# Three-product mix in float32 for the first batch, earlier transforms of the next batch, and a split load before the first product

## Chip, cores and metric

One NeuronCore of one Trainium2 chip runs the whole program. The metric is the device time in microseconds (us) of one execution. Times inside the program are microseconds from the start of the profiled execution's span.

## What is computed

```python
X = np.fft.rfft(x, axis=1)                 # x: 8 batches, 3072 rows, 256 channels, float32
Xr, Xi = X.real, X.imag
Yr = Xr @ w_r - Xi @ w_i + b_r             # the complex "mix", 256x256
Yi = Xr @ w_i + Xi @ w_r + b_i
Y  = softshrink(Yr, 0.01) + 1j * softshrink(Yi, 0.01)
y  = np.fft.irfft(Y, n=3072, axis=1)
out = ((y @ w_a) * (y @ w_b)) @ w_out      # w_a, w_b: 256x1536, w_out: 1536x256, 64-bit floats
```

`w_a`, `w_b` and `w_out` arrive as 64-bit floats; VectorE (DVE) and ScalarE (ACT) decode them from their 32-bit words inside the kernel.

## The kernel before

**Stages.** The transform of 3072 rows is factored in two steps (48 by 64). For each batch `b` the program has: `f1`, 16 tasks that multiply a block of `x` by a 96x96 matrix and store it to DRAM (`g_d`); `f2` and `f3`, 12 tasks each (index `u`), the second transform step and the mix; `i1`, 12 tasks, the first step of the inverse, stored to DRAM (`d_d`); and `i2`, which loads `d_d` back (`dt`) and makes the rows `yr` that enter the products. The products run over 32 pairs of row blocks and, in each, 12 blocks `j` of the hidden width; `step` does one `j`: seven products (Strassen-Winograd, `prod(p, j, k)`, k = 0 to 6) and four pieces of the projection (`proj`). Tasks of the next batch are put into two `slot()` places of each step.

**Number formats.** Batches 1 to 7 split each operand in a high and a low float32r part (`split`: ACT makes the high part, DVE or GpSimd (POOL) the low part) and multiply three times (`mm3`). Batch 0 goes in plain float32 on TensorE (PE), with one pass less of preparation: `f3_plain` multiplies the real and the imaginary part (`X[:, dh, i]`) each by a 512 column matrix (`wab`), and adds the bias by float32r products of `pick` with `bias_k` (tile name `early`).

**The startup** is everything before step 0: load, `f1` of batch 0, `f2`/`f3`/`i1` of batch 0, and meanwhile the decoding of four chunks of `w_a`, `w_b` (`in_weights`, tiles `w_t`, `w`, results `wc0` to `wc3`) and of four blocks of `w_out` (`out_weights(j)`, j = 0 to 3, results `wo0` to `wo3`). Each `out_weights(j)` is a chain: ACT takes the absolute value, six DVE operations, ACT casts the high part, and one more subtraction gives the low part.

**Order.** No engine reorders. The class `Order` decides in which order instructions are written to each engine: it keeps a planned time for PE and the other engines and writes an operation of a chain when its planned time has come. `od.put(c)` writes all that is left of chain `c` at once. `spare` chains are written only where the plan has room. `od.without = "G"` keeps POOL out of the choice.

**End of the startup.** After the last `i1`, PE runs 24 products whose result nobody reads (`busy(24, ...)`), then two `f1` tasks of batch 1 (`AHEAD = 2`), then `i2` of the first pair, then step 0. The loads of `dt` wait until the last block of `d_d` has landed. The four `w_out` blocks are all decoded before step 0.

Of the kernel before, what the change touches and what calls it, by code (L numbers as in the profile page):

```python
# [12 lines left out]
F32 = mybir.dt.float32  # L13
# [104 lines left out]
RING = 9  # L118
AHEAD = 2
LATE = 4  # L120
# [144 lines left out]
def fft_mix_glu_kernel(ctx: ExitStack, tc: tile.TileContext, x, w_r, w_i, b_r, b_i, w_a, w_b, w_out, c1, c1f, vf, m2, v, t2, c3, out):  # L265
# [72 lines left out]
    def load_mix():  # L338
        tmp = state["tmp"]
        wab = state["wab"] = [tmp.tile([P, 2, 2 * D], F32, name=f"wab{c}", bufs=1) for c in range(2)]  # L340
        v_f = state["v_f"] = tmp.tile([P, 2, P], F32, name="v_f", bufs=1)
        pick_in = tmp.tile([34, 3, P], F32, name="pick_in", bufs=1)
        bias_in = tmp.tile([34, D], F32, name="bias_in", bufs=1)
        wr, wi = (wab[0][:, :, D * k : D * (k + 1)] for k in range(2))
        wn, wr2 = (wab[1][:, :, D * k : D * (k + 1)] for k in range(2))
        for o, w in ((wr, w_r), (wi, w_i), (wr2, w_r)):
            nc.sync.dma_start(o, w.rearrange("(c p) e -> p c e", p=P))
        nc.vector.memset(bias_in, 0.0)
        nc.vector.memset(pick_in, 0.0)
        for k in (0, 32):  # L350
            for q, bq in enumerate((b_r, b_i)):
                nc.gpsimd.dma_start(bias_in[k + q : k + q + 1], bq[None, :])
            nc.gpsimd.dma_start(pick_in[k : k + 2], c3)
        nc.gpsimd.dma_start(v_f, vf)
        at = od.load(10 * P)
        return od.chain(
            ("A", 512, lambda e: nc.scalar.mul(wn, wi, -1.0)),
            ("AV", 3 * P, lambda e: copy(e, pick, pick_in)),
            ("A", D, lambda e: nc.scalar.copy(bias_k, bias_in)),
            ("V", D, lambda e: tt(e, bias_k[32:34], bias_in[32:34], bias_k[32:34].bitcast(F32), ALU.subtract)),  # L360
            spare=True,
            after=at,
        )

    def split_mix():
        w2, w3, v_in = (p1.tile([P, 2, D], F32, tag=t, name="w_in") for t in ("sxh", "sxl", "xs"))
        v_in = v_in.rearrange("p s (i n) -> p s i n", i=2)
        c1_in = state["tmp"].tile([R, 2, R], F32, name="c1_in", bufs=1)
        wr, wi = (state["wab"][0][:, :, D * k : D * (k + 1)] for k in range(2))
        nc.sync.dma_start(c1_in, c1)  # L370
        nc.sync.dma_start(v_in, v)
        for q, bq in enumerate((b_r, b_i)):
            nc.sync.dma_start(bias[:, q, :], bq[None, :].to_broadcast([P, D]))
        ops = [
            ("V", 512, lambda e: nc.vector.scalar_tensor_tensor(w3, wr, -1.0, wi, op0=ALU.mult, op1=ALU.subtract)),
            ("VG", 512, lambda e: tt(e, w2, wi, wr, ALU.subtract)),
            ("AV", 2 * R, lambda e: copy(e, c1_sb, c1_in)),
        ]
        for k, w in enumerate((wr, w2, w3)):
# [34 lines left out]
    def in_weights(first, last, raw_tile, w_tile, t_tile, deep=1):  # L414
# [26 lines left out]
        def combine(i):  # L441
# [19 lines left out]
            ops += parts((4, b11), (6, b12), (5, b22), (2, b21))  # L461
            chunks[c] = od.chain(*ops, ("S", 0, lambda e: out_weights(0) if c == LATE - 1 else None), spare=True)

# [15 lines left out]
    def out_weights(j):  # L479

        early = j < EARLY
        if j == 0:
            out_load(0)
        elif not early:
            od.put(wo_done[j - 1])
        if j != EARLY - 1:
            out_load(j + 1)
        raw = state.pop(("wo", j))
        if early:
            hi, lo = (p6.tile([P, W], F32, tag="yr", name="w_t")[:, :D] for _ in range(2))  # L490
            w = state["tmp"].tile([P, D], F32, tag="w", name="w", bufs=5)
        else:
            a = p1.tile([P, 2, D], F32, tag="zy", name="wo_a")
            b = p1.tile([P, 2, D], F32, tag="zc", name="wo_b")
            hi, lo, w = a[:, 0], a[:, 1], b[:, 0]
# [22 lines left out]
    def f1_pre(b, u):  # L518
# [6 lines left out]
        xs[b, u] = xh, xl, od.chain(*split(512, xi, xh, xl), after=t if b < 2 else 0.0)  # L525

    def busy(n, l, r):

        for _ in range(n):
            mm(bank[0][: l.shape[1], : r.shape[1]], l, r, True, True)  # L530

# [90 lines left out]
    def f2_plain(u, bk):  # L622

        X = state["tmp"].tile([P, 2, 2, P], F32, tag="ld", name="sf")
        ops = [("AV", 512, lambda e: copy(e, X.rearrange("p dh c n -> p (dh c n)"), bk))]
        Z = X
        if u == 0:
            Z = state["tmp"].tile([P, 2, 2, P], F32, tag="ld", name="sf0")

            def cut(e):  # L630
                nc.vector.tensor_copy(Z, X)
                nc.vector.memset(Z[:, :, :, 0:1], 0.0)

            ops.append(("V", 600, cut))
        c = od.chain(*ops, urgent=len(ops))
        od.reads(bk, c, len(ops) - 1)
        xs[0, u] = X, Z, c

# [3 lines left out]
    def f3_plain(u, i):  # L642
        X, Z, c = xs[0, u]
        if i == 0:
            bk = f3_ps[u] = od.bank()
            od.need(c)
        else:
            bk = f3_ps.pop(u)
        pa, pb = bk[:, 0:D], bk[:, D : 2 * D]
        wab = state["wab"]  # L650
# [4 lines left out]
        if u == 0:
            if i == 0:
                return
            for k, o in ((1, pb), (0, pa)):
                for c_ in range(2):
                    if c_:  # L660
                        biased(o, 2 * k)
                    for dh in range(2):
                        w = wab[c_][:, dh, D * k : D * (k + 1)]
                        mm(o, (X if c_ == k else Z)[:, dh, c_], w, c_ == dh == 0, c_ == dh == 1, skip_group_check=True)
        else:
            for dh in range(2):
                mm(bk, X[:, dh, i], wab[i][:, dh], i == dh == 0, i == dh == 1, skip_group_check=True)
            if i == 0:
                biased(pa, 0)
                biased(pb, 1)  # L670
                return
        xs.pop((0, u))
        if u > 1:
# [3 lines left out]
        lo, hi = slice(0, 64), slice(64, 128)  # L677
        take = [
            ("AV", D, lambda e, o=o, h=h, p=p, q=q: copy(e, y[o, h], p[q]))
            for o, p in ((hi, pb), (lo, pa))  # L680
            for h, q in enumerate((lo, hi))
        ]
        c = od.chain(
            *take,
            ("v", 512, lambda e: nc.vector.tensor_scalar(z, y, LAM, -LAM, op0=ALU.min, op1=ALU.max)),
# [182 lines left out]
    def proj(p, j, i):  # L868
# [183 lines left out]
    with tc.manual_schedule():  # L1052
# [5 lines left out]
        f1_loads(0)  # L1058
        mix = load_mix()
        in_weights(  # L1060
# [17 lines left out]
        ts = first_mid_tasks()  # L1078
        ts[-3] = after(ts[-3], lambda: [f1_loads(1), ms.extend(i2_matrix(0, th) for th in range(2))])
        tasks.extend(ts)  # L1080
        while tasks:
            slot()
        od.put(rest)
        busy(24, v_sb[:, 0, 1], wm_h[:, 0].rearrange("p i d -> p (i d)"))
        od.stored(2 * P)
        for th in range(2):
            i2_load(0, 0, th, ms[th])
        f1_start(1)
        for t in f1_tasks(1)[:AHEAD]:
            t()  # L1090
        for c in range(LATE):
            have(c)
        for j in range(EARLY):
            od.put(wo_done[j])
        od.spare_slack = 0.0
        startup.close()
        od.without, od.pace = "", 2.8
        state["ring"] = pool("ring", RING)
# [90 lines left out]
```

## Time and profile before

| | us |
|---|---|
| three timed runs | 2907.4, 2909.16, 2910.06; median 2909.16 |
| the profiled execution | 2907.86 |
| its span, first to last instruction | 2905.4 |
| PE busy in the span | 2855.6 (98%) |
| DVE, ACT, POOL busy | 1838.1, 1467.4, 817.6 |

The profiled execution is 1.3 us below the median, and 2.5 us of it lie outside the span. PE is busy for 98% of the span, so time is to be had or lost where PE waits or repeats work; the page shows this in the first two of its 40 slices, which are the startup. The table says nothing of single waits; these are in the rows below.

### The profile page before, as it was taken

What the parts mean: (1) busy time and instruction counts of PE and PEld (TensorE: products, weight loads), DVE (VectorE), ACT (ScalarE), POOL (GpSimd) and SP (SyncE); (2) the same over time, 40 slices, a digit from 0 to 9 for tenths busy, and PEclk for the clock granted to TensorE, in tenths of its full rate; (3) what the DMA queues carried; (4) which work ended last, traced back from release to release, by engine and by line L of the source; (5) the groups of instructions that cost most, each with busy time, mean ns of one, the idle gap of its engine ahead of it and who ended that gap; (6) DMA issues with size and microseconds to landing.
All of it is one profiled execution on the core that took longest, in us unless ns stands there. A gap on an engine that the chain in (4) does not pass through costs nothing.

```text
span 2905.4 us, 46403 instructions
## 1 busy us (share of the span) xinstructions
PE 2855.6 (98%) x16837; PEld 2653.8 (91%) x16837; DVE 1838.1 (63%) x3670; ACT 1467.4 (51%) x3205; POOL 817.6 (28%) x762
## 2 busy tenths in 40 slices
PE   6899999999999999999999999999999999999999
PEld 3599999999999999999999999999999999999998
DVE  6776666566666666566665666656666566666665
ACT  4554555545455444545446444464454545444444
POOL 1132332223322323323323233133332233310000
PEclk8999999999999999999999999999999999999999
DMA  7531212211132111321113211131111311110000
GB/s 243 149 99 41 63 37 89 78 38 60 41 100 75 49 44 53 100 63 51 40 58 100 63 54 37 59 98 60 58 40 55 109 45 59 37 52 22 21 12 23
DMA packets 122965, 187.02 MB, mean 64 GB/s; under 512 B 12652, under 2 KB 81360, under 8 KB 122736
## 3 DMA queue, kind: packets, MB, share of 16 engines
q1 hardware_dynamic: 120784, 176.54, 20.0%
q0 software_dynamic: 1840, 7.48, 0.9%
q8 instruction: 132, 2.16, 0.3%
q14 instruction: 97, 0.79, 0.1%
q10 hardware_dynamic: 112, 0.04, 0.0%
HBM read 108.52 MB, written 75.50 MB: 63 GB/s over the span
## 4 chain that ended last, share of the span: by engine, by line
PE 90%; ACT 2%; POOL 1%; DVE 1%; issue 1%; DVEq 0%; ACTq 0%; POOLq 0%
PE bank L299 90%; ACT s L947 1%; DVE bank L293 1%; POOL sx L293 0%; POOL ycl L293 0%; ACT xs L290 0%; POOL xs L293 0%; ACT osb L290 0%; ACT g L922 0%; DVE s L293 0%; ACT zh L408 0%; ACT sx L594 0%; ACT sx L597 0%; ACT g L984 0%; ACT yr L290 0%
## 5 line engine op out<-in xcount | busy, mean ns | idle before, releaser
L293 DVE TENSOR_TENSOR bank<-bank,s 128x384 f32<-128x384 f32 x1152 | 648.6, 563 | 662.6 <-PE bank L299 557.9
L947 ACT COPY s<-bank 128x384 f32<-128x384 f32 x1152 | 549.2, 485 | 210.0 <-PE bank L299 200.3
L984 ACT CAST g<-bank 128x384 fp32r<-128x384 f32 x384 | 184.5, 480 | 830.2 <-DVE s L293 439.0
L293 DVE TENSOR_TENSOR g<-bank,g 128x384 fp32r<-128x384 f32 x768 | 425.8, 556 | 171.0 <-ACT g L984 143.2
L293 DVE TENSOR_TENSOR s<-bank,s 128x384 f32<-128x384 f32 x768 | 423.6, 552 | 12.5 <-PE bank L299 0.8
L293 POOL TENSOR_TENSOR ycl<-yr,ych 128x384 fp32r<-128x384 f32 x194 | 203.2, 1071 | 691.9 <-ACT ych L408 691.5
L922 ACT CAST g<-bank 128x384 fp32r<-128x384 f32 x384 | 184.4, 480 | 214.2 <-DVE bank L293 213.2
L293 POOL TENSOR_TENSOR zy<-zy,zc 128x512 f32<-128x512 f32 x84 | 107.8, 1283 | 544.3 <-DVE zc L742 537.2
L293 POOL TENSOR_TENSOR x<-xin,x 96x512 fp32r<-96x512 f32 x109 | 144.0, 1323 | 397.2 <-ACT x L408 209.5
L299 PE MATMUL bank<-ych,wc0l 128*128 128x384 f32 x672 | 233.0, 347 | 7.2 <-ACT s L947 5.9
L299 PE MATMUL bank<-ych,wc3l 128*128 128x384 f32 x672 | 235.5, 350 | 0.4
L299 PE MATMUL bank<-ych,wc2l 128*128 128x384 f32 x672 | 232.7, 346 | 0.0
L299 PE MATMUL bank<-ych,wc1l 128*128 128x384 f32 x672 | 230.7, 343 | 0.6
L299 PE MATMUL bank<-ycl,wc0h 128*128 128x384 f32 x672 | 226.8, 338 | 0.5 <-POOL ycl L293 0.5
L299 PE MATMUL bank<-ych,wc3h 128*128 128x384 f32 x672 | 226.6, 337 | 0.0
L299 PE MATMUL bank<-ycl,wc2h 128*128 128x384 f32 x672 | 226.6, 337 | 0.0
L299 PE MATMUL bank<-ych,wc2h 128*128 128x384 f32 x672 | 226.5, 337 | 0.0
L299 PE MATMUL bank<-ych,wc0h 128*128 128x384 f32 x672 | 226.5, 337 | 0.0
L299 PE MATMUL bank<-ycl,wc3h 128*128 128x384 f32 x672 | 226.5, 337 | 0.0
L299 PE MATMUL bank<-ycl,wc1h 128*128 128x384 f32 x672 | 226.2, 337 | 0.0
L299 PE MATMUL bank<-ych,wc1h 128*128 128x384 f32 x672 | 226.1, 336 | 0.0
L299 PE MATMUL bank<-wm_h,sx 128*128 128x256 f32 x1008 | 191.3, 283 | 5.1 <-POOL sx L293 5.1
(197 smaller groups left out, 6423.1 us busy)
## 6 DMA issues: line engine op xcount, KB each, us to landing
xin<-in_x_dram SPq DMA_DIRECT2D x128, 192.0 KB, 2.9
g_d<-gst SPq DMA_DIRECT2D x128, 192.0 KB, 2.1
gt<-g_d SPq DMA_DIRECT2D x96, 256.0 KB, 2.8
d_d<-dst SPq DMA_DIRECT2D x96, 256.0 KB, 2.1
dt<-d_d SPq DMA_DIRECT2D x64, 384.0 KB, 4.1
out_dram<-osb SPq DMA_DIRECT2D x64, 384.0 KB, 2.6
m_in<-const_m_dram SPq DMA_DIRECT2D x96, 128.0 KB, 2.1
t_in<-const_t_dram SPq DMA_DIRECT2D x64, 144.0 KB, 2.4
```

The source lines that it names most:

```text
L293: (nc.vector if e == "V" else nc.gpsimd).tensor_tensor(o, a, b, op=op)
L299: nc.tensor.matmul(o, lhsT=l, rhs=r, start=start, stop=stop, **kw)
L922: ("A", W, lambda e: nc.scalar.copy(h, X)),
L947: return s, od.chain(("A", W, lambda e: nc.scalar.copy(s, q[:, :W])), urgent=1)
L984: ("A", W, lambda e: nc.scalar.copy(h1, Y)),
```

## The change

It has five parts.

1. The mix of batch 0 uses three products for a complex multiplication in place of four: `(Xr+Xi) w_r` (its copy on ACT is `k`), `Xr (w_i - w_r)` and `Xi (-w_r - w_i)`, each of 256 columns. DVE makes the sum `Xr+Xi` (`ss`) and adds `k` when it takes two of the four result blocks out of PSUM.
2. `w_r` and `w_i` are loaded once each, by POOL's DMA queue behind the first `w_a`, `w_b` blocks, instead of three loads by SP. The two differences (`w23`) are made in `load_mix` and used again in `split_mix`.
3. `AHEAD` goes from 2 to 6: six `f1` tasks of batch 1 stand before `i2`. The four next ones (`GAP`) go together into the first slot of step 0. `busy` is gone.
4. `dt` is loaded in two parts: rows 0 to 79, and rows 80 to 95, which the last two `i1` tasks write.
5. `out_weights(0)` is started only after the `dt` loads, and `w_out` blocks 0 to 3 are finished by `out_have`, called from step 0 (through `out_weights(4)`), not before `i2`. POOL stays out of the choice until the first pair's parts are split.

```diff
-AHEAD = 2
+AHEAD = 6
+GAP = 4
...
     def load_mix():
...
-        for o, w in ((wr, w_r), (wi, w_i), (wr2, w_r)):
-            nc.sync.dma_start(o, w.rearrange("(c p) e -> p c e", p=P))
+        for o, w in ((wr, w_r), (wi, w_i)):
+            nc.gpsimd.dma_start(o, w.rearrange("(c p) e -> p c e", p=P))
...
     def out_weights(j):
...
         if j == 0:
             out_load(0)
-        elif not early:
-            od.put(wo_done[j - 1])
-        if j != EARLY - 1:
-            out_load(j + 1)
+        else:
+            out_have(j - 1)
+        out_load(j + 1)
...
+    def out_have(j):
+        while j not in wo_done:
+            od.put(wo_done[max(wo_done)])
+        od.put(wo_done[j])
...
     def f3_plain(u, i):
...
+        if i == 0:
+            bk = od.bank()
+            pa, pb = bk[:, 0:D], bk[:, D : 2 * D]
+            od.need(c)
+            product(pa, Xs, wri[:, 0], True, True)
+            k = p1.tile([P, D], F32, tag="k", name="k")
+            ck = od.chain(("A", D, lambda e: nc.scalar.copy(k, pa)), urgent=1)
+            mm(pb, X[:, 0, 0], w23[:, 0, 0], False, False, skip_group_check=True)
+            biased(pb, 1 + (u == 0))
+            mm(pb, X[:, 1, 0], w23[:, 0, 1], False, u > 0, skip_group_check=True)
...
+        od.need(ck)
+        biased(pa, 0)
+        product(pa, X[:, :, 1], w23[:, 1], False, True)
...
         c = od.chain(
-            *take,
+            ("V", D, lambda e: tt(e, y[hi, 0], pb[lo], k[lo], ALU.add)),
+            ("V", D, lambda e: tt(e, y[hi, 1], pb[hi], k[hi], ALU.add)),
+            ("AV", D, lambda e: copy(e, y[lo, 0], pa[lo]), 3),
+            ("AV", D, lambda e: copy(e, y[lo, 1], pa[hi])),
...
-        busy(24, v_sb[:, 0, 1], wm_h[:, 0].rearrange("p i d -> p (i d)"))
         od.stored(2 * P)
+        first = [p2.tile([R, 4, D], F32, tag="dt", name="dt") for th in range(2)]
+        for rows in (slice(0, 80), slice(80, R)):
+            for th in range(2):
+                nc.sync.dma_start(first[th][rows].rearrange("p n d -> p (n d)"), d_d[0][rows, 4 * D * th : 4 * D * (th + 1)])
         for th in range(2):
-            i2_load(0, 0, th, ms[th])
-        f1_start(1)
-        for t in f1_tasks(1)[:AHEAD]:
+            dt[0, 0, th] = first[th], ms[th], od.load(6 * R)
+        out_weights(0)
+        ahead = f1_tasks(1)
+        for t in ahead[:AHEAD]:
             t()
...
-        for j in range(EARLY):
-            od.put(wo_done[j])
```

The order in which instructions stand shows what this moves. On PE, one task of the mix (u = 2; `m_in,gt` is `f2`, `zy,v_f` is `i1`, `early` the bias) reads before:

```order
L299 MATMUL bank_80<-wab_148,sf 128x512 x2
L299 MATMUL bank_80<-early 128x256 x2
L299 MATMUL bank_81<-zy,v_f 128x256 x2
L299 MATMUL bank_80<-wab_149,sf 128x512 x2
L299 MATMUL bank_82<-m_in,gt 128x2x64 x4
```

and now:

```order
L300 MATMUL bank_80<-wri,ss 128x256 x2
L300 MATMUL bank_80<-w_160,sf 128x256
L300 MATMUL bank_80<-early 128x256
L300 MATMUL bank_80<-w_160,sf 128x256
L300 MATMUL bank_81<-zy,v_f 128x256 x2
L300 MATMUL bank_80<-early 128x256
L300 MATMUL bank_80<-w_160,sf 128x256 x2
L300 MATMUL bank_82<-m_in,gt 128x2x64 x4
```

Four products of 512 columns became six of 256, and the two bias products, which stood together, now stand apart. On ACT, from the last casts of the first pair's rows (`ych`) into step 0 (`s` is the first eviction of a product, `x` the cast for an `f1` task, `gst` the eviction of one), the order was:

```order
L408 CAST ych<-yr 128x384 x5
L947 COPY s<-bank_81 128x384
L408 CAST x<-xin 96x512 x2
L393 ACTIVATE wo_a<-wo_raw 128x256
L290 COPY gst<-bank_85 96x512
L947 COPY s<-bank_81 128x384
```

and is now:

```order
L404 CAST ych<-yr 128x384 x5
L404 CAST wo0h<-wo_b 128x256
L389 ACTIVATE wo_a<-wo_raw 128x256
L404 CAST wo1h<-wo_b 128x256
L389 ACTIVATE wo_a<-wo_raw 128x256
L404 CAST wo2h<-wo_b 128x256
L389 ACTIVATE wo_a<-wo_raw 128x256
L404 CAST wo3h<-wo_b 128x256
L943 COPY s<-bank_81 128x384
L404 CAST x<-xin 96x512 x2
L389 ACTIVATE wo_a<-wo_raw 128x256
L291 COPY gst<-bank_85 96x512 x2
```

The `w_out` blocks 1 to 3 came to stand between the last cast and the first eviction. On POOL, from its first computation on, the order was (`ycl` are low parts of the first pair's rows, `x` those of `f1` tasks):

```order
L293 ISA
L293 TENSOR_TENSOR ycl<-yr,ych 128x384 x4
L293 TENSOR_TENSOR x<-xin,x 96x512 x2
L293 TENSOR_TENSOR wo4l<-wo_b,wo4h 128x256
L293 TENSOR_TENSOR x<-xin,x 96x512 x2
L293 TENSOR_TENSOR wo5l<-wo_b,wo5h 128x256
```

and is now:

```order
L294 ISA
L294 TENSOR_TENSOR wo0l<-wo_b,wo0h 128x256
L473 DMA wo_raw<-in_moe_w_out_dram 128x512
L294 TENSOR_TENSOR wo1l<-wo_b,wo1h 128x256
L473 DMA wo_raw<-in_moe_w_out_dram 128x512
L294 TENSOR_TENSOR wo2l<-wo_b,wo2h 128x256
L294 TENSOR_TENSOR wo3l<-wo_b,wo3h 128x256
L294 TENSOR_TENSOR x<-xin,x 96x512 x7
L294 TENSOR_TENSOR wo5l<-wo_b,wo5h 128x256
```

The low parts of `wo0` to `wo3` and the loads of blocks 2 and 3 came ahead of the first `x` part, which belongs to the seventh `f1` task.

## Rows read from the trace of the kernel before

**Rows 1.** The page's first line.

```profile
span 2905.4 us, 46403 instructions
```

**Rows 2.** Busy time, clock and DMA of stretches: engine busy us, clock share, DMA share.

```profile
46.50:112.00 65.50, 65.50 (x227) 34.77 (x227) 54.23 (x120) 42.95 (x99) 4.52 (x8) 1.00 0.45 136
112.00:115.50 3.50, 0.89 (x3) 0.06 (x1) 1.21 (x3) 1.94 (x5) 0.00 (x0) 1.00 0.96 281
...
130.67:137.70 7.03, 1.18 (x4) 0.40 (x3) 5.95 (x8) 3.93 (x9) 5.21 (x4) 0.54 0.66 173
137.70:141.40 3.70, 3.70 (x10) 3.22 (x11) 1.96 (x6) 2.06 (x4) 0.00 (x0) 0.50 0.52 148
```

**Rows 3.** Timeline of PE in the mix: start, us, instruction, count.

```profile
48.41 0.38 PE L299 MATMUL bank<-early 34*128 34x256 f32 x1
48.72 1.13 PE L299 MATMUL bank<-wab,sf 128*128 128x256 f32 x4
49.69 1.05 PE L299 MATMUL bank<-m_in,gt 128*128 128x128 f32 x8
...
57.35 0.50 PE L299 MATMUL bank<-early 34*128 34x256 f32 x2
57.77 1.13 PE L299 MATMUL bank<-zy,v_f 128*128 128x256 f32 x4
58.74 1.88 PE L299 MATMUL bank<-wab,sf 128*128 128x512 f32 x4
60.46 1.05 PE L299 MATMUL bank<-m_in,gt 128*128 128x128 f32 x8
```

**Rows 4.** Waits of SP's DMA queue, 10 to 32 us.

```profile
SPq L551 <- DMA wab<-in_w_r_dram: 2.6, 2, 1.4
```

**Rows 5.** Timeline of PE from the last inverse task into step 0.

```profile
116.09 6.05 PE L299 MATMUL bank<-wm_h,v_sb 128*128 128x512 f32 x24
...
124.29 3.81 PE L299 MATMUL bank<-t_in,dt 96*128 96x96 f32 x32 [0.78 <-DMA dt<-d_d]
...
134.95 1.17 PE L299 MATMUL bank<-x,c_sb 96*96 96x512 f32 x2 [4.27 <-ACT x L408]
...
138.23 0.53 PE L299 MATMUL bank<-ych,wc0l 128*128 128x384 f32 x1
...
145.06 0.87 PE L299 MATMUL bank<-x,c_sb 96*96 96x512 f32 x3
145.76 0.34 PE L299 MATMUL bank<-ych,wc0l 128*128 128x384 f32 x1
```

**Rows 6.** Timeline of SP's queue and landings of `x` blocks, 95 to 160 us.

```profile
119.49 0.79 SPq L785 DMA_DIRECT2D dt<-d_d  x2
DMA to landing us min/median/max: 2.5/3.2/5.6
```

**Rows 7.** Timeline of ACT around the last mix task and the `ych` casts.

```profile
118.34 1.12 ACT L408 CAST x<-xin 96x512 fp32r<-96x512 f32 x2
...
131.84 2.16 ACT L408 CAST ych<-yr 128x384 fp32r<-128x384 f32 x5 [2.09 <-DVE yr L293]
```

**Rows 8.** Timeline of DVE: end of the mix, one `w_out` block, first `wo4` operation.

```profile
114.72 0.69 DVE L293 TENSOR_TENSOR zy<-zy,zc 128x512 f32<-128x512 f32 x1
115.33 0.29 DVE L398 TENSOR_SCALAR w_t<-w_t 128x256 f32<-128x256 f32 x1
...
118.12 0.43 DVE L293 TENSOR_TENSOR wo1l<-w,wo1h 128x256 fp32r<-128x256 f32 x1 [0.47 <-ACT wo1h L408]
...
136.45 1.35 DVE L398 TENSOR_SCALAR wo_a<-wo_a 128x256 f32<-128x256 f32 x1
```

**Rows 9.** Timeline of POOL, 100 to 150 us.

```profile
135.94 1.71 POOL L293 TENSOR_TENSOR x<-xin,x 96x512 fp32r<-96x512 f32 x1
...
142.71 0.72 POOL L293 TENSOR_TENSOR wo4l<-wo_b,wo4h 128x256 fp32r<-128x256 f32 x1
```

**Rows 10.** Landings of `w_out` loads issued by POOL, 100 to 127 us.

```profile
DMA to landing us min/median/max: 3.0/3.1/3.1
```

More of the change, by code (lines that the diff above doesn't have):

```diff
@@ L339, in load_mix @@
         tmp = state["tmp"]
-        wab = state["wab"] = [tmp.tile([P, 2, 2 * D], F32, name=f"wab{c}", bufs=1) for c in range(2)]
+        wri = state["wri"] = tmp.tile([P, 2, 2, D], F32, name="wri", bufs=1)
+        w23 = state["w23"] = tmp.tile([P, 2, 2, D], F32, name="w23", bufs=1)
         v_f = state["v_f"] = tmp.tile([P, 2, P], F32, name="v_f", bufs=1)
@@ L343, in load_mix @@
         bias_in = tmp.tile([34, D], F32, name="bias_in", bufs=1)
-        wr, wi = (wab[0][:, :, D * k : D * (k + 1)] for k in range(2))
-        wn, wr2 = (wab[1][:, :, D * k : D * (k + 1)] for k in range(2))
-        for o, w in ((wr, w_r), (wi, w_i), (wr2, w_r)):
-            nc.sync.dma_start(o, w.rearrange("(c p) e -> p c e", p=P))
+        wr, wi = wri[:, 0], wri[:, 1]
+        for o, w in ((wr, w_r), (wi, w_i)):
+            nc.gpsimd.dma_start(o, w.rearrange("(c p) e -> p c e", p=P))
         nc.vector.memset(bias_in, 0.0)
@@ L354, in load_mix @@
         nc.gpsimd.dma_start(v_f, vf)
-        at = od.load(10 * P)
+        at = od.load(8 * P)
         return od.chain(
-            ("A", 512, lambda e: nc.scalar.mul(wn, wi, -1.0)),
+            ("V", 512, lambda e: nc.vector.scalar_tensor_tensor(w23[:, 1], wr, -1.0, wi, op0=ALU.mult, op1=ALU.subtract)),
+            ("V", 512, lambda e: tt(e, w23[:, 0], wi, wr, ALU.subtract)),
             ("AV", 3 * P, lambda e: copy(e, pick, pick_in)),
@@ L365, in split_mix @@
     def split_mix():
-        w2, w3, v_in = (p1.tile([P, 2, D], F32, tag=t, name="w_in") for t in ("sxh", "sxl", "xs"))
-        v_in = v_in.rearrange("p s (i n) -> p s i n", i=2)
+        v_in = p1.tile([P, 2, 2, P], F32, tag="xs", name="v_in")
         c1_in = state["tmp"].tile([R, 2, R], F32, name="c1_in", bufs=1)
-        wr, wi = (state["wab"][0][:, :, D * k : D * (k + 1)] for k in range(2))
         nc.sync.dma_start(c1_in, c1)
@@ L373, in split_mix @@
             nc.sync.dma_start(bias[:, q, :], bq[None, :].to_broadcast([P, D]))
[L374 to L379, printed above, removed]
+        ops = [("AV", 2 * R, lambda e: copy(e, c1_sb, c1_in))]
+        for k, w in enumerate((state["wri"][:, 0], state["w23"][:, 0], state["w23"][:, 1])):
             ops += [
@@ L461, in combine @@
             ops += parts((4, b11), (6, b12), (5, b22), (2, b21))
-            chunks[c] = od.chain(*ops, ("S", 0, lambda e: out_weights(0) if c == LATE - 1 else None), spare=True)
+            chunks[c] = od.chain(*ops, spare=True)
         for i in range(deep):
@@ L483, in out_weights @@
             out_load(0)
-        elif not early:
-            od.put(wo_done[j - 1])
-        if j != EARLY - 1:
-            out_load(j + 1)
+        else:
+            out_have(j - 1)
+        out_load(j + 1)
         raw = state.pop(("wo", j))
[L489 to L495, printed above, removed]
+        a = p1.tile([P, 2, D], F32, tag="zy", name="wo_a")
+        b = p1.tile([P, 2, D], F32, tag="zc", name="wo_b")
+        hi, lo, w = a[:, 0], a[:, 1], b[:, 0]
         ops = [*decode(D, raw, hi, lo, w), *split(D, w, *wo[j])]
@@ L525, in f1_pre @@
         xs[b, u] = xh, xl, od.chain(*split(512, xi, xh, xl), after=t if b < 2 else 0.0)
-    def busy(n, l, r):
-        for _ in range(n):
-            mm(bank[0][: l.shape[1], : r.shape[1]], l, r, True, True)
     def f1(b, u):
@@ L624, in f2_plain, with real @@
         X = state["tmp"].tile([P, 2, 2, P], F32, tag="ld", name="sf")
-        ops = [("AV", 512, lambda e: copy(e, X.rearrange("p dh c n -> p (dh c n)"), bk))]
-        Z = X
-        if u == 0:
[L628 to L634, printed above, removed]
+        Xs = p1.tile([P, 2, P], F32, tag=("sxh", "sxl")[u % 2], name="ss")
+        sp = None
+        ops = [
+            ("AV", 512, lambda e: copy(e, X.rearrange("p dh c n -> p (dh c n)"), bk)),
+            ("V", 256, lambda e: tt(e, Xs, X[:, :, 0], X[:, :, 1], ALU.add)),
+        ]
+        if u == 0:
+            sp = p1.tile([P, 2, P], F32, tag="zc", name="s0")
+            def real(e):
+                nc.vector.memset(sp, 0.0)
+                nc.vector.tensor_tensor(sp[:, :, 0:1], X[:, :, 1, 0:1], X[:, :, 0, 0:1], op=ALU.subtract)
+                nc.vector.tensor_copy(Xs[:, :, 0:1], X[:, :, 0, 0:1])
+                nc.vector.memset(X[:, :, :, 0:1], 0.0)
+            ops.append(("V", 600, real))
         c = od.chain(*ops, urgent=len(ops))
         od.reads(bk, c, len(ops) - 1)
-        xs[0, u] = X, Z, c
+        xs[0, u] = X, Xs, sp, c
     f3_ps = {}
@@ L642, in f3_plain, with product @@
     def f3_plain(u, i):
[L643 to L650, printed above, removed]
+        X, Xs, sp, c = xs[0, u]
+        wri, w23 = state["wri"], state["w23"]
+        def product(o, x, w, start, stop):
+            for dh in range(2):
+                mm(o, x[:, dh], w[:, dh], start and dh == 0, stop and dh == 1, skip_group_check=True)
         def biased(o, k):
             mm(o, pick[:, k], bias_k, False, False, skip_group_check=True)
[L655 to L671, printed above, removed]
+        if i == 0:
[8 more added lines that the diff above has]
+            mm(pb, X[:, 1, 0], w23[:, 0, 1], False, u > 0, skip_group_check=True)
+            if u == 0:
+                product(pb, sp, wri[:, 0], False, True)
+            f3_ps[u] = bk, k, ck
+            return
+        bk, k, ck = f3_ps.pop(u)
+        pa, pb = bk[:, 0:D], bk[:, D : 2 * D]
+        od.need(ck)
+        biased(pa, 0)
+        product(pa, X[:, :, 1], w23[:, 1], False, True)
         xs.pop((0, u))
@@ L677, in f3_plain @@
         lo, hi = slice(0, 64), slice(64, 128)
[L678 to L682, printed above, removed]
         c = od.chain(
-            *take,
+            ("V", D, lambda e: tt(e, y[hi, 0], pb[lo], k[lo], ALU.add)),
+            ("V", D, lambda e: tt(e, y[hi, 1], pb[hi], k[hi], ALU.add)),
+            ("AV", D, lambda e: copy(e, y[lo, 0], pa[lo]), 3),
+            ("AV", D, lambda e: copy(e, y[lo, 1], pa[hi])),
             ("v", 512, lambda e: nc.vector.tensor_scalar(z, y, LAM, -LAM, op0=ALU.min, op1=ALU.max)),
@@ L876, in proj @@
         if p == 0:
+            out_have(j)
             od.need(wo_done[j])
@@ L1058, in fft_mix_glu_kernel @@
         f1_loads(0)
-        mix = load_mix()
         in_weights(
@@ L1067, in fft_mix_glu_kernel @@
         )
+        mix = load_mix()
         tasks.extend(f1_tasks(0))
@@ L1078, in fft_mix_glu_kernel @@
         ts = first_mid_tasks()
-        ts[-3] = after(ts[-3], lambda: [f1_loads(1), ms.extend(i2_matrix(0, th) for th in range(2))])
+        ts[-3] = after(ts[-3], lambda: [f1_loads(1), ms.extend(i2_matrix(0, th) for th in range(2)), f1_start(1)])
         tasks.extend(ts)
@@ L1092, in fft_mix_glu_kernel @@
             have(c)
-        for j in range(EARLY):
-            od.put(wo_done[j])
         od.spare_slack = 0.0
         startup.close()
-        od.without, od.pace = "", 2.8
         state["ring"] = pool("ring", RING)
@@ L1110, in fft_mix_glu_kernel @@
             yr_split(0, k, 3)
-        out_load(EARLY)
         for k in range(7):
             od.put(yc[0, k][2])
+        od.without, od.pace = "", 2.8
         for o in [*o_ps[1:], *x_ps, ya, yb]:
@@ L1131, in fft_mix_glu_kernel @@
                     if more:
-                        work += f1_tasks(b + 1)[0 if b else AHEAD :]
+                        work += f1_tasks(b + 1) if b else [lambda: [t() for t in ahead[AHEAD : AHEAD + GAP]], *ahead[AHEAD + GAP :]]
                     else:
```

## The prediction, made before the result was known

> **What bounds the kernel now.** I read the page first: the span is 2905.4 us [rows 1], and the profiled execution took 2907.86, so 2.5 us lie around it. Then I cut the startup into stretches [rows 2]. From 46.50 to 112.00 PE is busy for every one of 65.50 us, and DVE for 54.23 of them: the mix of the first batch is bound by PE. Behind it the picture turns. [...] The timeline says what it waits for [rows 5]: 0.78 us for the load of `dt`, 4.27 for ACT's cast of an `x` block. The other PE time that yields nothing are the 24 unread products, 6.05 us. So there are two places to gain: fewer columns in the mix, and the waits and fillers between the last mix task and the third product (k = 2) of step 0, which starts at 138.23. I measure the latter from T, the end of the last DVE operation of the mix, at 115.41 (114.72 + 0.69 [rows 8]): k = 2 starts at T + 22.8.
>
> **Startup loads: -1.0.** Three loads of 256 KB become two, and leave SP's queue, where stores of `g_d` waited 2.6 us for them [rows 4]. Bounds: nothing, if other bytes take the room, and -2.6. I take -1.0, nearer to nothing, because I think that bytes and not order fill the queue, and only a third of the bytes of those three loads disappears. The two `w23` operations move into a time in which DVE waits for ACT and cost nothing; without that cover they would cost 1.4.
>
> **The mix: -5.** By columns, four times 512 against six times 256 saves a quarter. The rows say less [rows 3]. Two products of 512 columns take 1.72 us start to start (58.74 to 60.46), two of 256 take 0.97 (48.72 to 49.69), not 0.86. Two bias products together take 0.42 (57.35 to 57.77), one alone 0.31 (48.41 to 48.72). Before: 2 x 1.72 + 0.42 = 3.86, and 0.10 where the first product follows the second transform; after: 3 x 0.97 + 2 x 0.31 = 3.53. That saves 0.43 to 0.45 in each of tasks 1 to 11; task 0 has eight products of 256 columns in both. 11 x 0.45 = 5.0; the bounds are 0.33 x 11 = 3.6 and, by columns alone, 0.86 x 11 = 9.5. DVE gains 36 operations (12 sums, 24 additions of `k`) at some 0.42, the length of its other operations of 256 columns [rows 8]: 15 us, and is rid of about 13 (the first `w_out` block, the differences, the tail of chunk 3, which now stand elsewhere), so 56 to 57 us of 60.5. It stays hidden behind PE. The new wait, PE's second half of a task for ACT's copy `k`, lies behind one to two microseconds of other products and costs nothing; uncovered it would be half a microsecond per task. So T moves by -6.0 with the loads.
>
> **From T to the first product: +4 to +5.** Before, `i2` starts at 124.29 = T + 8.9, with only the load of `dt` to wait for. Now six `f1` tasks stand ahead of it on PE. SP issues in order: the first `x` block beyond the three already loaded comes behind the four `dt` loads, and the second pair of these waits for the last `d_d` to land. That was at 119.49 [rows 6], T + 4.1; two issues take 0.79, so this `x` leaves at T + 4.9 and lands, at the median of 3.2, at T + 8.1. Then three casts and two evictions alternate on ACT, each 0.56 to 0.61 [rows 7], the low part of each `x` is DVE's, and the sixth `f1` ends near T + 12.5. The split load itself, some 1.5 us earlier, is hidden behind this and brings nothing; without the `f1` tasks in front it would bring that much. Bounds: T + 10.5, when the block lands at 2.5 and DVE's own queue (13 us of leftover `wc3` and `x` work) is the limit, and T + 15 with a landing at 5.6.
>
> At which clock `i2` runs is not in the trace. Before, the clock held over a stretch in which PE worked 0.89 us of 3.50 (112.00 to 115.50, 1.00) and fell in one of 4.27 [rows 2, 5]. Between the third and the fourth `f1` PE will wait about 3.5 us, after several shorter gaps. I take half speed for the first part of `i2`, as in 137.70 to 141.40, where 3.70 us of dense work did 1.85 us' worth: +1.9; the bounds are 0 and 3.8, the length of `i2` [rows 5]. So `i2` ends near T + 18.2. [...]
>
> **From the first product to k = 2: the `w_out` blocks.** Before, the casts `ych` end at 134.00 (131.84 + 2.16 [rows 7]), 9.7 us behind the start of `i2`. POOL no longer disturbs them, so I take 8.0 + 1.9 for the clock: T + 22.4. The first two products run at about T + 19, then PE waits. ACT's next instructions are the cast of `wo0`, then absolute value and cast of `wo1`, `wo2` and `wo3`, each behind six DVE operations, and only then the eviction `s` of the first product, on which k = 2 waits, and the `x` cast of the seventh `f1`, which stands on PE ahead of k = 2. Before, this was done while `dt` was on its way. One block took 2.32 us of DVE (115.33 to 118.12 - 0.47), 0.47 for the cast [rows 8], and I take as much for the absolute value of the same block: 3.3 with hops. Blocks 2 and 3 are also loaded late: POOL issues each load behind the low part of the block two before, 0.72 [rows 9], and it lands 3.1 later [rows 10]; this adds about 0.9 in all. Three blocks 9.9, the load 0.9, cast of `wo0` 0.4, eviction and `x` cast 1.1: 12.3. The seventh `f1` starts at T + 34.7. Bounds: 9 (no load late, no hop) and 17 (DVE held behind POOL each time, as in the 1.35 us of an operation that takes 0.29 [rows 8, 9], and loads slow).
>
> Four `f1` follow on one PSUM bank. Each waits for the eviction of the one before, 0.6, and runs 1.4 at half clock (0.70 at full, 145.06 to 145.76 [rows 5]); three need a low part from POOL, 1.71 in the one that the rows show [rows 9], 1.3 by my estimate where no DVE work lies beside it, and two wait for it. 2.0 + 2.0 + 2.8 + 2.5 = 9.3. So k = 2 starts at T + 44.0 against T + 22.8: +21.2. At that point ten `f1` are done and not three; seven at 0.70 are 4.9 saved in later steps.
>
> **Sum.** -1.0 - 5.0 + 21.2 - 4.9 = +10.3. The profiled execution would take 2918.2; it lies 1.3 below the median of the three runs, so the median would be 2919.5.
>
> **Rivals.** *The decode is out of the way.* If engines reach `wo1` to `wo3` before the `ych` casts end, the 12.3 us vanish, and k = 2 starts at T + 30 or so: 10.3 - 12.3 - 2 = -4, about 2905 us, and not slower. For it speaks that DVE idles while it waits for the late `x`; against it that ACT, DVE and POOL take instructions in order and these stand behind the last `ych`. It decides as soon as the seventh `f1` starts within 4 us of the last `ych`. *The mix gains by columns.* Then -9.5 in place of -5.0: +5.8, 2915. The 0.97 of rows 3 speaks against it. *The clock holds.* Then 1.9 less, and up to 2 less in the four `f1`: +7, 2916; the stretch from 112.00 speaks for it, the wait of 4.27 us against. *DVE bounds the mix*, if its 57 us and waits exceed 60.5 by 3: +13, 2922.5; that DVE waits for ACT in every task speaks for it, its spare 3.5 us against.
>
> **Chances.** The sum 0.58, with its own range 2914 to 2925; the clock 0.13; columns 0.09; decode out of the way 0.12; DVE 0.08. A measurement of this kernel tells 0.2%, 5.8 us, from no change: 2903.3 to 2915.0. Slower takes most of the sum, the clock, DVE and half of columns, 0.74; the same takes some of the sum's lower end, half of columns and over half of the first rival, 0.17; faster 0.09. The range is 2909 to 2926: it leaves out the first rival, and some 4 in 100 above.
>
> **What would show it.** Right: PE's stretch of f2, f3 and i1 about 5 us shorter with no waits; `i2` waits for an `f1` whose `x` part is late and not for `dt`; PE idle for 14 to 16 us behind the second product, ended by ACT's `x` or `s`; ACT and DVE alternating on `wo` tiles in it; low clock until after the four `f1`. Wrong: a first eviction of step 0 right behind its product, or a task period of the mix near 5.0 us in place of 5.4.

## The result, and the profile after

The changed kernel takes 2947.9 us (median of 4 runs, 2946.6 to 2949.1) against 2909.05: ratio 1.0134, 95% interval 1.0116 to 1.0152. I had forecast 2919.5, in 2909 to 2926. The sign was right; the loss is 38.9 us and not 10.5.

Its profiled execution has a span of 39.4 us more than that of [rows 1]. The page's first line:

```profile
span 2944.8 us, 46491 instructions
```

I cut both spans at three points which the timelines show: the start of the mix's first product, T (the end of the last DVE operation on `zy`), and the start of the third product of step 0 (k = 2). The line that ends at T in the changed kernel (129.79 + 0.69 = 130.48):

```profile
129.79 0.69 DVE L294 TENSOR_TENSOR zy<-zy,zc 128x512 f32<-128x512 f32 x1
```

| stretch | before | after | difference | forecast |
|---|---|---|---|---|
| start of the mix | 44.48 | 46.59 | +2.1 | -1.0 |
| mix to T | 70.93 | 83.89 | +13.0 | -5.0 |
| T to k = 2 | 22.8 | 47.7 | +24.9 | +21.2 |
| behind k = 2 | 2767.2 | 2766.6 | -0.6 | -4.9 |
| sum | | | +39.4 | +10.3 |

So the big term was near, and 18.0 of the 29.1 us that are missing lie in the mix, which was to become faster.

**The mix.** PE, which never waited there before [rows 2, 3], now waits in every task. One period of the timeline (start, busy us, instruction, count, idle before and its releaser):

```profile
91.12 0.38 PE L300 MATMUL bank<-early 34*128 34x256 f32 x1 [1.59 <-ACT k L656]
91.43 0.70 PE L300 MATMUL bank<-w,sf 128*128 128x256 f32 x2
91.97 1.02 PE L300 MATMUL bank<-zy,v_f 128*128 128x512 f32 x2
92.92 0.38 PE L300 MATMUL bank<-early 34*128 34x256 f32 x1
93.23 1.13 PE L300 MATMUL bank<-w,sf 128*128 128x256 f32 x4
94.20 1.05 PE L300 MATMUL bank<-m_in,gt 128*128 128x128 f32 x8
95.09 1.03 PE L300 MATMUL bank<-wri,ss 128*128 128x256 f32 x4
95.96 0.59 PE L300 MATMUL bank<-w,sf 128*128 128x256 f32 x2
98.10 0.38 PE L300 MATMUL bank<-early 34*128 34x256 f32 x1 [1.54 <-ACT k L656]
```

The period is 98.10 - 91.12 = 6.98 us; in the timeline of before it is 5.81:

```profile
84.60 1.88 PE L299 MATMUL bank<-wab,sf 128*128 128x512 f32 x4
...
90.41 1.88 PE L299 MATMUL bank<-wab,sf 128*128 128x512 f32 x4
```

In the changed kernel PE stops at a bias product (`early`), with only one product, `w,sf`, between it and the product `wri,ss` that `k` copies. What ACT does meanwhile, in its order:

```profile
95.99 0.37 ACT L291 COPY zy<-bank 64x256 f32<-64x256 f32 x1 [1.91 <-DVE zy L294]
96.26 0.58 ACT L291 COPY sf<-bank 128x512 f32<-128x512 f32 x1
96.86 0.37 ACT L291 COPY zy<-bank 64x256 f32<-64x256 f32 x1
97.14 0.51 ACT L404 CAST wc2h<-w 128x384 fp32r<-128x384 f32 x1
97.67 0.37 ACT L656 COPY k<-bank 128x256 f32<-128x256 f32 x1
```

ACT comes to `k` only after the next task's `sf`, two copies of the last task and a weight cast. The waits of PE from the mix's start to T (us in total, times, longest):

```profile
PE bank L300 <- ACT k L656: 13.6, 12, 1.9
```

Stretches (busy us of PE, PEld, DVE, ACT, POOL; clock share; DMA share, GB/s):

```profile
46.59:62.35 15.76, 13.44 (x40) 9.35 (x41) 9.81 (x23) 5.33 (x12) 1.08 (x2) 0.70 0.22 60
62.35:115.15 52.80, 43.45 (x195) 30.41 (x194) 40.09 (x90) 23.85 (x55) 2.71 (x6) 1.00 0.43 127
...
154.40:168.45 14.05, 0.00 (x0) 0.00 (x1) 10.32 (x25) 5.57 (x15) 4.28 (x6) 0.50 0.32 93
168.45:178.20 9.75, 6.80 (x13) 2.93 (x14) 4.72 (x9) 4.42 (x9) 4.80 (x4) 0.50 0.42 126
```

No engine is full in the mix: of 52.80 us PE is busy for 43.45 and DVE for 40.09. It is a chain of waits, and not a bound by an engine's work.

**The start.** The second transforms of tasks 0 and 1 end at 37.1 now (the last one ended at 44.2 before), yet the first product of the mix starts at 46.59. PE's line of before, and of now:

```profile
44.48 1.77 PE L299 MATMUL bank<-wab,sf 128*128 128x256 f32 x4 [0.26 <-issue]
```

```profile
46.59 2.04 PE L300 MATMUL bank<-wri,ss 128*128 128x256 f32 x4 [9.47 <-issue]
```

ACT's timeline says why: the copy `sf` of task 0, on which all else waits, stands behind casts that wait for DVE and for a weight block that lands late.

```profile
39.74 0.51 ACT L404 CAST wc0h<-w 128x384 fp32r<-128x384 f32 x1 [2.95 <-DVE w L294]
41.52 0.56 ACT L389 ACTIVATE w_t<-wraw 128x384 f32<-128x384 f32 x1 [1.26 <-DMA wraw<-in_moe_w_b_dram]
...
42.79 0.57 ACT L291 COPY sf<-bank 128x512 f32<-128x512 f32 x1
```

`sf` ends at 43.36. The sum `ss`, which the first product reads, then stands behind weight decoding on DVE until 45.52, and the last write into it, which only task 0 has, ends at 46.48:

```profile
45.52 0.42 DVE L294 TENSOR_TENSOR ss<-sf 128x256 f32<-128x256 f32 x1
```

**T to k = 2.** The timeline of PE, to be read beside [rows 5], and of ACT from the last `ych` on:

```profile
130.63 1.43 PE L300 MATMUL bank<-zy,v_f 128*128 128x512 f32 x2 [2.60 <-DVE zy L294]
131.16 4.03 PE L300 MATMUL bank<-x,c_sb 96*96 96x512 f32 x6
...
140.80 2.45 PE L300 MATMUL bank<-x,c_sb 96*96 96x512 f32 x5 [3.72 <-ACT x L404]
...
145.42 6.97 PE L300 MATMUL bank<-t_in,dt 96*128 96x96 f32 x32
152.10 0.67 PE L300 MATMUL bank<-ych,wc0l 128*128 128x384 f32 x1
...
168.45 1.17 PE L300 MATMUL bank<-x,c_sb 96*96 96x512 f32 x2 [14.08 <-ACT x L404]
...
178.20 0.52 PE L300 MATMUL bank<-ych,wc0l 128*128 128x384 f32 x1
```

```profile
154.13 2.17 ACT L404 CAST ych<-yr 128x384 fp32r<-128x384 f32 x5 [1.22 <-DVE yr L294]
156.20 0.40 ACT L404 CAST wo0h<-wo_b 128x256 fp32r<-128x256 f32 x1
...
159.98 0.41 ACT L404 CAST wo1h<-wo_b 128x256 fp32r<-128x256 f32 x1 [3.04 <-DVE wo_b L294]
...
163.60 0.41 ACT L404 CAST wo2h<-wo_b 128x256 fp32r<-128x256 f32 x1 [2.47 <-DVE wo_b L294]
...
167.10 0.41 ACT L404 CAST wo3h<-wo_b 128x256 fp32r<-128x256 f32 x1 [2.62 <-DVE wo_b L294]
167.41 0.47 ACT L943 COPY s<-bank 128x384 f32<-128x384 f32 x1
167.78 1.14 ACT L404 CAST x<-xin 96x512 fp32r<-96x512 f32 x2
```

This is the stall that was forecast, block by block: PE does nothing for 14.05 us, until the four blocks are done and ACT comes to `s` and to the seventh `x`.

### The profile page after: what moved, and what is told of

It is laid out like the page before. It is cut to its first block, busy times and chain, and to the rows that moved or that the text cites. A ratio compares the mean times of both kernels' runs of the same rounds, so it can differ in the third digit from the quotient of the medians.

```text
span 2944.8 us, 46491 instructions
## 1 busy us (share of the span) xinstructions
PE 2862.5 (97%) x16857; PEld 2666.8 (91%) x16857; DVE 1859.4 (63%) x3714; ACT 1465.5 (50%) x3192; POOL 810.9 (28%) x758
## 4 chain that ended last, share of the span: by engine, by line
PE 86%; ACT 3%; DVE 2%; POOL 2%; issue 1%; DVEq 0%; ACTq 0%; POOLq 0%
PE bank L300 86%; ACT s L943 1%; DVE bank L294 1%; POOL sx L294 1%; DVE zy L294 0%; POOL zl L294 0%; ACT xs L291 0%; POOL ycl L294 0%; DVE s L294 0%; POOL xs L294 0%; ACT zh L404 0%; ACT g L980 0%; ACT g L918 0%; ACT osb L291 0%; ACT ych L404 0%
```

## The experiments

Times are medians of the runs; T, k = 2 and the waits are from the profile of each.

**e1_two_banks**: the two products that follow get a PSUM bank (one of the tiles `bank` into which PE writes) apart from the one that `k` reads.

```diff
-            bk = od.bank()
-            pa, pb = bk[:, 0:D], bk[:, D : 2 * D]
+            bk, bb = od.bank(), od.bank()
+            pa, pb = bk[:, 0:D], bb[:, D : 2 * D]
...
-            mm(pb, X[:, 0, 0], w23[:, 0, 0], False, False, skip_group_check=True)
+            mm(pb, X[:, 0, 0], w23[:, 0, 0], True, False, skip_group_check=True)
...
         od.reads(bk, c, 2)
+        od.reads(bb, c, 4)
```

> The changed kernel, with the second and third of Gauss's products of a mix task in a PSUM bank of their own, so that the bias product behind ACT's copy k no longer touches the bank that k reads. Theory A (the mix is slow because PE stops at that bias product until ACT, whose queue is in order, comes to k: 1.5 us in each of tasks 2 to 11 and 2.3 us in the first two): the wait shrinks to under 0.4 us a task, the period from 6.6 or 7.0 to about 5.5 us, the end of the mix moves from 130.5 to 113 to 119, and the time falls by 12 to 17 us, to 2931 to 2936. Rival B (ACT and DVE together are the bound of a task, and k is only where it shows): the wait moves to another product, the period stays over 6.3 us, the time falls by less than 4 us.

2927.7 us, 20.2 less. The period is 5.36 and PE waits for `k` nowhere. Timeline of PE in one task and to the same product of the next:

```profile
86.12 1.03 PE L300 MATMUL bank<-wri,ss 128*128 128x256 f32 x4
86.99 0.59 PE L300 MATMUL bank<-w,sf 128*128 128x256 f32 x2
87.51 0.38 PE L300 MATMUL bank<-early 34*128 34x256 f32 x1
...
91.48 1.03 PE L300 MATMUL bank<-wri,ss 128*128 128x256 f32 x4
```

T is at 114.6, 15.9 earlier, and k = 2 is earlier by as much; 2.7 more came behind k = 2, which I have not traced. Theory A, with a larger gain than it gave; B falls.

**e2_wout_early**: the first four `w_out` blocks as before (begun at the end of chunk 3, tiles of their own), and

```diff
         for c in range(LATE):
             have(c)
+        for j in range(EARLY):
+            od.put(wo_done[j])
```

> The changed kernel, with the first four w_out blocks decoded as in the kernel before: begun behind the last chunk, into tiles of their own, and put on the queues ahead of the inverse's evictions. Theory A (the stall of 14.1 us behind the second product is the decode that stands between the last ych cast and the first eviction s on ACT, DVE and POOL): the stall falls to under 4 us, but part of the decode now stands ahead of the ych casts, so the time falls by 5 to 12 us, to 2936 to 2943. Rival B (the stall is waiting for late x blocks and the fall of the clock): it stays over 10 us, and the time within 3 us of 2948.

2940.3, 7.6 less, as A has it. But the stall did not vanish. It moved ahead of the first product:

```profile
160.21 0.69 PE L300 MATMUL bank<-ych,wc0l 128*128 128x384 f32 x1 [7.62 <-ACT ych L404]
```

k = 2 gains only 4.1 (174.10); the other gain lies behind it and was not traced. As long as all four blocks are decoded in this stretch, the place of the decoding decides which product waits for it, not whether one waits.

**e4_mix_only** and **e5_mix_two_banks**: the kernel before with the new mix alone, and with that mix in two banks. The edits are those of the change's diff in `load_mix` (but the loads left on SP, ahead of the chunk weights), `split_mix`, `f2_plain` and `f3_plain`, and for e5 that of e1. Of `load_mix`:

```diff
-        for o, w in ((wr, w_r), (wi, w_i), (wr2, w_r)):
+        for o, w in ((wr, w_r), (wi, w_i)):
             nc.sync.dma_start(o, w.rearrange("(c p) e -> p c e", p=P))
```

> The kernel before, with the mix of the first batch by three products alone (its two loads where the three stood, on SP's queue; everything else as before). Theory A (the mix loses by the wait for k): 11 tasks with 1.2 to 1.5 us more, less some 0.5 us saved: the mix ends 8 to 13 us later than 115.4, the time is 2917 to 2923. By the prediction's row (-5.0 for the mix, -1.0 for the loads): 2903. By columns alone: 2899.

> The kernel before, with the mix by three products alone and the second and third of them in a bank of their own. Theory A (without the wait for k the rows' sum holds: 0.45 us saved in each of 11 tasks): the mix ends 3 to 6 us earlier than 115.4, the time is 2903 to 2906. Rival B (ACT's and DVE's queues bound it): the time is 2910 or more.

e4: 2923.5, ratio 1.0049 (1.0034 to 1.0064) to the kernel before; 12 waits for `k`, 13.7 us, T at 121.65. e5: 2908.2, ratio 0.9998 (0.9989 to 1.0007), no wait for `k`. The mix takes 79.80 us in e4 and 66.16 in e5: 13.6 apart, the sum of the waits. Before it took 70.93, so without the wait it is 4.8 shorter, and T is at 106.93, 8.5 earlier than before. But in both kernels k = 2 starts 32.1 behind T, where it was 22.8, and e5's time is that of before: it missed what I expected, 2903 to 2906. So did e4: its T came earlier than the 123.4 to 128.4 that I had expected, and its time lies just above the 2923. In e5 DVE's last `w_out` block ends at 129.62, 2.2 later than the 127.39 of before, though the mix ends 8.5 earlier: before, the first of the four blocks was decoded inside the mix, and now all four stand behind it. The low part of the first block, before and in e5:

```profile
106.81 0.43 DVE L293 TENSOR_TENSOR wo0l<-w,wo0h 128x256 fp32r<-128x256 f32 x1 [0.47 <-ACT wo0h L408]
```

```profile
119.79 0.42 DVE L293 TENSOR_TENSOR wo0l<-w,wo0h 128x256 fp32r<-128x256 f32 x1 [0.47 <-ACT wo0h L403]
```

Step 0 of e5 waits for the last block (DVE, then PE):

```profile
129.20 0.42 DVE L293 TENSOR_TENSOR wo3l<-w,wo3h 128x256 fp32r<-128x256 f32 x1 [0.47 <-ACT wo3h L403]
```

```profile
130.87 0.69 PE L299 MATMUL bank<-ych,wc0l 128*128 128x384 f32 x1 [10.69 <-ACT ych L403]
```

What PE wins in the mix is lost to DVE and ACT behind it.

**e3_ahead2**: in the changed kernel,

```diff
-AHEAD = 6
-GAP = 4
+AHEAD = 2
+GAP = 0
```

> The changed kernel with two transforms f1 of the next batch ahead of the inverse, as in the kernel before, and none in the gap behind the second product. Theory A (the six f1 hold the inverse back by an x block that comes late, and the four of the gap stand one behind the other on one bank at half clock, 9.8 us from 168.45 to 178.20, for work that costs 0.7 us each elsewhere): i2 starts some 6 us earlier, k = 2 some 14 us earlier, eight f1 at 0.7 come back later, so the time falls by 6 to 12 us, to 2936 to 2942. Rival B (the f1 only fill time in which PE waits for DVE and ACT anyway): the time is the same or up to 5 us longer.

2932.9, 15.0 less: A, and more than it gave. `i2` starts 6.1 earlier (6 expected) and k = 2 16.1 earlier (14 expected). What I had set too large is the loss of the eight transforms behind it: from k = 2 to the end it takes 2769.0 against 2766.6, so 2.4 and not 5.6, as far as two profiles can tell.

**e6_load_order**: in the changed kernel, the loads of the mix on SP, ahead of the chunk weights.

```diff
-            nc.gpsimd.dma_start(o, w.rearrange("(c p) e -> p c e", p=P))
+            nc.sync.dma_start(o, w.rearrange("(c p) e -> p c e", p=P))
...
+        mix = load_mix()
         in_weights(
...
-        mix = load_mix()
```

> The changed kernel with the two loads of the mix's weights on SP's queue and ahead of the chunk weights, where the three stood before. Theory A (with the loads behind the chunk weights on POOL's queue the first copy sf stands on ACT behind casts that wait for late weight blocks, so the first product of the mix comes at 46.6 though both second transforms end at 37.1): the mix starts at 41 to 43, and the time falls by 3 to 6 us, to 2942 to 2945. Rival B (the mix waits for the weights of the chunks wherever its own loads stand, or the 5 us are lost again behind the mix): less than 2 us.

2940.1, 7.8 less, and the mix starts without a wait behind the second transforms:

```profile
37.61 3.75 PE L300 MATMUL bank<-m_in,gt 128*128 128x128 f32 x16 [12.50 <-DMA gt<-g_d]
41.38 1.22 PE L300 MATMUL bank<-wri,ss 128*128 128x256 f32 x4
```

A for the place; the gain is some 2 us over it. With two loads for three the mix starts at 40.8 to 42.5 in all kernels that load them first, against 44.48 before: two loads for three go with a start that is 1.9 to 3.7 earlier, though no run changes their number alone; their new queue and place, which e6 undoes together, cost 5.2.

**e7_three_undone**: e1, e2 and e6 together.

> The changed kernel with three edits together: a bank of their own for the second and third product, the first four w_out blocks decoded early, and the loads of the mix in their old place. Theory A (the three losses add up): 2947.9 - 20.2 - 7.6 - 4.5 = 2915.6, between 2912 and 2919. Rival B (once the mix is shorter, DVE's queue of weight decoding bounds the stretch, as in the kernel before with the mix in two banks, where PE was 8.5 us earlier at the end of the mix and the time the same): the gains overlap, and the time is 2920 to 2927.

2919.4: 28.5 less, of 35.6 by adding. Just above A's range and below B's. Up to k = 2, which starts at 151.62, the gains add up: 26.6 us, where e1, e2 and e6 have 15.9, 4.1 and 7.1. Most of what is missing lies behind k = 2, which I have not traced. PE waits 7.6 us for `ych` as in e2, so this wait is no sign of the overlap that B names.

**e8_two_early_blocks**: e5 with two blocks of `w_out` decoded ahead of step 0, and each further one two blocks ahead of its use.

```diff
-EARLY = 4
+EARLY = 2
```

> The kernel before with the mix by three products in two banks, and two w_out blocks decoded early in place of four (the others each two products ahead of their use). Theory A (DVE's decoding, 3.1 us a block in a row up to 129.6, is what the first products of step 0 wait for there, so the mix's gain of 5 us on PE was lost to it): two blocks fewer, the first product comes 5 to 6 us earlier, and the time falls by 3 to 6 us, to 2902 to 2905. Rival B (the decoding waits on PE's way wherever it stands): the same 2908, within 1.5 us.

2904.6, ratio 0.9982 (0.9972 to 0.9992). The first product starts at 125.17, 5.7 earlier than in e5: A.

**e9_four_undone**: e7 with the edit of e3.

> The changed kernel with four edits together: the mix in two banks, early w_out blocks, the old place of the loads, and two f1 ahead of the inverse with none in the gap. What is left of the change is the mix by three products, the dt load in two parts and the missing filler. Theory A (the four parts are the whole loss): the time is that of the kernel before with the mix in two banks, 2908, within 3 us. Rival B (the load in two parts, or the missing filler with the clock it held, costs something of its own): 2912 or more.

2905.8, ratio 0.9991 (0.9982 to 1.0000): A. The load of `dt` in two parts and the missing filler cost nothing that shows; within the interval the four parts are the whole loss.

**e10_one_early_block**: e5 with `EARLY = 1`.

> The kernel before with the mix in two banks and one w_out block decoded early (2904.6 with two, 2908.2 with four). Theory A (DVE's decoding still bounds the start of step 0, 3.1 us a block): the first product comes some 2 to 3 us earlier than 125.2, and the time is 2901 to 2904. Rival B (PE's chain to the inverse is now the later one, or the blocks are missed in step 0): 2904 to 2908.

2901.85, ratio 0.9980 (0.9971 to 0.9989): A, and by 0.2% faster than the kernel before. The first product comes at 121.54, and PE waits 1.27 for it where e5 waited 10.69:

```profile
121.54 0.69 PE L299 MATMUL bank<-ych,wc0l 128*128 128x384 f32 x1 [1.27 <-ACT ych L403]
```

**e11_no_filler**: e8 without the filler, whose products nobody reads.

```diff
-        busy(24, v_sb[:, 0, 1], wm_h[:, 0].rearrange("p i d -> p (i d)"))
```

> The kernel before with the mix in two banks and two early blocks, without the 24 unread products. Theory A (they stand beside the decoding on DVE and ACT, which the first product waits for by 4.4 us, so taking them away brings nothing and lets the clock fall): the inverse runs at half clock, the time is 2904 to 2908. Rival B (they are on the path): the first product comes 3 us or more earlier, the time is 2899 to 2902.

2904.75, as e8: A. The inverse takes 7.14 us in place of 3.71, near the 6.97 that it takes at a clock of 0.50 in the changed kernel, and starts 0.4 earlier; the first product, which waits for `ych` in both (2.92 us, and 4.41 in e8), comes 1.5 later (126.67 against 125.17).

**e12_before_two_early**: the kernel before with `EARLY = 2`.

> The kernel before, with two early w_out blocks in place of four, and nothing else. Theory A (its start of step 0 is bound by decoding too, but PE's mix ends only 3 us before): a little is won, 2905 to 2908. Rival B (there PE's own chain is the later one, so that fewer blocks bring nothing): 2908 to 2910. If it falls to 2904, the gain with the mix in two banks is that of the blocks alone.

2906.0, ratio 0.9990 (0.9981 to 0.9999): A, a little. By the medians, 2.9 against 5.7, about half of e8's gain is that of the blocks alone, but the intervals of the two overlap. At the start of k = 2 the share is larger: 138.23 before, 134.25 here, 133.33 in e8, so 4.0 of 4.9. No run has the old mix with one early block, so what the new mix adds to e10 is open.

## Why the prediction was wrong, by its steps

**The mix: -5 forecast, +13.0 measured; the step that failed.** The sum of products was right: without the wait e5's mix is 4.8 shorter, and e1's period is 5.36 for 5.81, the 0.45 of the sum. What failed is the sentence that the wait for `k` "lies behind one to two microseconds of other products and costs nothing; uncovered it would be half a microsecond per task". Both halves of it were wrong. I looked for the wait where the second half of the task accumulates onto what `k` has copied. The program waits earlier: `k` reads one half of a bank, and the next product into the other half of the same bank already waits for ACT. The order of the instructions shows it, with `k` put on ACT's queue between the two products `w` (the brackets name the engine whose signal an instruction waits for; `Activation` is ACT):

```
L300 MATMUL bank_82<-wri,ss 128x256 [waits DVE_49]
L300 MATMUL bank_82<-wri,ss 128x256
L300 MATMUL bank_82<-w_160,sf 128x256
L300 MATMUL bank_82<-early 128x256 [waits Activation_49]
L300 MATMUL bank_82<-w_160,sf 128x256
```

The two lines with `w_160,sf` are the two halves of the second product, and the first of them (0.59 us in the timeline) is all that covers the wait. That the wait goes with the shared bank, e1 and e5 show: with the later products in a bank of their own PE waits for `k` nowhere, where it waits 12 times in the change (13.6 us) and 12 times in e4 (13.7 us). And its length is not that of a copy (0.37 us): `k` stands on ACT behind up to three copies and a cast, in the task shown from 95.99 to 97.67. The waits are 13.6 us in 12 tasks, 1.1 each; e1's mix is 16.4 shorter than that of the change, 13.6 of it these waits. The other 2.8 I put down, without a run of its own, to the half clock at the mix's start: the change has 0.50 from 46.59 to 55.00, e1 a mean of 0.65 from 47.14 to 53.93 and 1.00 behind it. My bounds, -3.6 to -9.5, held no loss, though I had named the wait. That the mix would be bound by DVE, a rival, is refuted: in e1 PE is busy for all 57.07 us from 53.93 to 111.00, and DVE for 52.82 of them. But DVE's queue bounds the start of step 0 once the mix is short (e5).

**Startup loads: -1.0 forecast, +2.1 measured.** The step has two parts of opposite sign. Two loads for three go with a gain larger than I took (1.9 to 3.7; my bounds were nothing and 2.6). The part I left out is that the loads now stand on another queue behind the weights of the chunks, so that `sf` waits behind casts on ACT and `ss` behind decoding on DVE: 5.2.

**T to k = 2: +21.2 forecast, +24.9 measured.** Right in its parts. Between T and the steps, forecast and measured: `i2` starts 12.5, 14.9; first products 19, 21.6; seventh `f1` 34.7, 38.0; k = 2 44.0, 47.7. From the end of the last `ych` cast (156.30) to the seventh `f1`, 12.3 forecast, it is 12.15; PE's own wait, 14 to 16 forecast, is 14.05; the four `f1`, 9.3, are 9.75. So the decode was priced rightly, and the term that was too small is the half clock, ahead of the first product. I charged 1.9 us, my estimate from 137.70 to 141.40 [rows 2], for a part of `i2`, but all of `i2` ran at half (6.97 for 3.81 in [rows 5]), and so did most of the six `f1` ahead of it (0.55 from 130.63 to 137.10): the last three take 4.6 us (140.80 to 145.42), where 0.70 each would be 2.1. The clock is 0.50 from 140.80 to 182.36. The rival that the clock holds is refuted.

**The credit: -4.9 forecast, -0.6 measured.** Seven `f1` done early leave PE 0.70 us each later only where PE is busy without a gap. In step 0 they also fill its waits, as I read it: e3 against the change says 2.4 for eight. Neither 0.6 nor 2.4 is sharp, since among kernels with ten `f1` done by k = 2 (the change, e1, e2, e6, e7) this stretch takes 2763.9 to 2766.7. A part of the waits stands in 220 to 240 of the change, where PE works 18.45 of 20 us and DVE 16.87 with the last `w_out` blocks; the rest was not traced.

**The rival on the other side** (the decode is out of the way, 2905) priced the decode at 12.3 if it were earlier. e2 did that and won 7.6, 4.1 of it ahead of k = 2: the queue of DVE and ACT has the same work either way.

## What to carry to other kernels

When an edit lets another engine read half of a PSUM bank, look for the first later product into that bank, not for the first that needs the result, and price the wait by what stands ahead on the reader's queue (here 1.1 us in each of 12 tasks, for a copy of 0.37). If the wait is in a loop, give the later products a bank of their own (e1: 20.2 us less). Before counting the gain of a shorter stage, ask which engine's queue ends it next: here 4.8 us of TensorE were worth nothing in e5, where the decoding of four blocks ends the stretch, and what gained was fewer blocks in it (e8, e10). Work that was moved within such a stretch mostly changed who waits: e2 took the idle 14.05 us behind the second product away, and PE waited 7.62 us ahead of the first.

## What was unexpected of the hardware

The same wait of 2.60 us behind the mix leaves the clock alone in one kernel and halves it in another. Ahead of it both had worked without a gap at 1.00 (e8 from 100.00 to 104.50, e5 from 100.00 to 103.70), and behind it both run the same filler. Stretches of e8, then of e5, just behind the wait (columns as above, the clock is the third number from the end):

```profile
107.92:110.00 2.08, 2.08 (x7) 1.40 (x8) 1.94 (x5) 0.94 (x2) 0.00 (x0) 1.00 0.03 8
```

```profile
107.08:109.00 1.92, 1.92 (x4) 1.05 (x5) 1.78 (x5) 0.30 (x1) 0.00 (x0) 0.62 0.04 9
109.00:111.00 2.00, 2.00 (x6) 1.54 (x5) 1.90 (x5) 1.62 (x4) 0.00 (x0) 0.51 0.38 130
```

By 111 to 114 e5 is back at 1.00. The kernel before and e12, whose PE instructions are the same up to there, differ alike behind a wait of 2.67: the two products `zy,v_f` right behind it take 1.10 us before and 2.04 in e12, and the clock is 1.00 in the kernel before from 116.09 to 118.00. And in the mix of the changed kernel waits of up to 1.59 us in every task leave the clock at 1.00 (62.35 to 115.15). A sum for this program that charges half clock to a stretch behind a wait of this length is a guess.
